# Attention two items at a time, with the softmax's reciprocals applied to its output

## The chip, the cores and the metric

The kernel runs on one core of a Trainium2 chip. The metric is the device time of one execution in microseconds. The profile is one execution taken by the hardware profiler; its engines are PE (matrix products), DVE (VectorE), ACT (ScalarE), POOL (GpSimd) and SP, which issues the transfers. PE has a second row in the profile, PEld, for its weight loads.

## The reference

Attention over 4 batches of 8 heads, 576 positions of 64 numbers, with rotary embedding of queries and keys; its output, as 2304 tokens of 512 numbers, goes through two dense blocks of 512 to 2048 to 512.

```python
q_rot, k_rot = rotate(q), rotate(k)
scores = q_rot @ k_rot.T / sqrt(64)
scores = scores - max(scores)                # per row
attn = exp(scores)
attn = attn / (sum(attn) + 1e-9)
x = (attn @ v) as (2304, 512)
h = x @ w1_in;  g = h if h > 0 else exp(h) - 1;  x = g @ w1_out
h = x @ w2_in;  g = h - tanh(h);                 out = g @ w2_out
```

All is float32.

## The kernel before, in words

**Attention** works on 16 pairs of heads. A pair is cut into nine items: for each of four blocks of 128 query rows (u = 0 to 3) one item for the first head (h = 0) and one for the second (h = 1), and a ninth item (h = None) that holds the last 64 rows of both heads. An item is 128 rows of 576 scores.

The loop (lines 377 to 409) takes one item a turn. In turn i it emits, in this order: loads that are due, the row maximum of item i on DVE (`emit_max`, line 216), copies out of PSUM that earlier transposes left (`flush`, lines 256 to 275, two of five on DVE, three on ACT), the scores of item i + 1 on PE (`emit_s`, line 207), the exponential of item i on ACT with the row sums as a by-product (`emit_exp`, line 230), the normalization of item i - 1 (`emit_norm`: an add of 1e-9 and a reciprocal on DVE, lines 242 and 243, and for each head a multiplication of 128 x 576 on POOL, line 246), preparation of the next pairs, the transposes of item i - 4 on PE (`emit_t`, line 293; a remainder of 64 columns of both heads together, line 307, or line 300 for the ninth item), and matmuls with v into the output (`emit_pv`, line 325). Outputs are made for row blocks 0 and 1, 2 and 3, and the ninth item, 256, 256 and 64 columns wide, in five chunks each. Every engine executes its own instructions in the order of emission.

**PSUM** has eight banks: two score tiles of two banks (`ps_s`), two tiles for transposes (`ps_t`), two for outputs (`ps_v`).

**Preparation** (`prep`, lines 132 to 163) turns the loaded q (x = 0) or k (x = 1) of a pair into a rotated copy, in five steps: two products with the tables of cosines and sines (POOL, line 142, for most), their sum (DVE, line 144), a rounded high half (ACT, line 147), and the low half, what the rounding left (DVE, line 152). Then `place` (lines 174 and 177) copies both halves by transfers on SP's queue to the tiles that the scores read: k in four copies, two for each head. A table (`early`, and the offsets in the line that makes `when`) says in which turn each step is emitted. For k the sum, the high half and the low half are due in turns 2, 3 and 4 of the pair before, and the scores of the pair's first two items are emitted in that pair's turns 8 and 9.

**Weights** of the dense blocks arrive as pairs of words and are converted in five parts (`conv_w`), for the first eight tiles during attention.

**The dense blocks** (from line 415) take 192 steps: 12 matmuls of `emit_f1` (line 442) and 12 of `emit_f2` (lines 498, 500) each, with activations, and splits into high and low halves on ACT and POOL, between them. They read the layer's input as a high half `xh` and a low half `xl`. Attention fills these directly: ACT rounds the output in PSUM to `xh` (line 273) and DVE subtracts to `xl` (line 265). Sums over the groups of the hidden dimension go to `acc`.

Of the kernel before, what the change touches and what calls it, by code (L numbers as in the profile page):

```python
# [8 lines left out]
F32 = mybir.dt.float32  # L9
# [14 lines left out]
def attention_elu_tanhshrink(ctx: ExitStack, tc: tile.TileContext, qk, v, w1i, w1o, w2i, w2o, tab, out):  # L24
# [22 lines left out]
    xh = const.tile([128, KC, NTOK], F32R, name="xh")  # L47
    xl = const.tile([128, KC, NTOK], F32R, name="xl")
# [52 lines left out]
    with ExitStack() as actx:  # L101
# [10 lines left out]
        tabs = acst.tile([128, 2, S], F32, name="tabs")  # L112
        zero = acst.tile([128, 64], F32, name="zero")
# [5 lines left out]
        def load_qk(p, x):  # L119
            if p == 1 and x == 0:  # L120
                t = p3.tile([128, 2, S], F32, tag="a", name="t0")
            else:
                t = (p1, p2)[x].tile([128, 2, S], F32, tag=f"t{x}", name=f"t{x}")
            nc.sync.dma_start(out=t, in_=qk[p, :, 2 * x:2 * x + 2, :])
            t_t[p, x] = t
# [6 lines left out]
        def prep(p, x, i):  # L132
            t = t_t[p, x]
            mul = SCALE if p > 0 and x == 0 else 1.0
            if i < 2:
# [4 lines left out]
                else:  # L140
                    eng = nc.vector if p < 2 and i == 1 else nc.gpsimd
                    eng.tensor_tensor(out=t[:, i, :], in0=t[:, i, :], in1=tabs[:, i, :], op=ALU.mult)  # L142
            elif i == 2:
                nc.vector.tensor_tensor(out=t[:, 0, :], in0=t[:, 0, :], in1=t[:, 1, :], op=ALU.add)  # L144
            elif i == 3:
                hl_t[p, x] = p1.tile([128, 2, S], F32R, tag=f"hl{x}", name=f"hl{x}")
                nc.scalar.mul(hl_t[p, x][:, 0, :], t[:, 0, :], mul)
# [87 lines left out]
        def emit_norm(i):  # L235
# [15 lines left out]
        late, late_x, late_l = [], [], []  # L251
# [4 lines left out]
        def flush():  # L256
# [7 lines left out]
            for x0, hp, o, n in late_l:  # L264
                nc.vector.tensor_tensor(
                    out=xl[:, hp, x0:x0 + n], in0=o[:, 0:n], in1=xh[:, hp, x0:x0 + n].bitcast(F32),
                    op=ALU.subtract,
                )
            late_l.clear()
            for p, grp, o, n in late_x:  # L270
                b, hp = divmod(p, 4)
                x0 = b * S + 256 * grp
                nc.scalar.copy(out=xh[:, hp, x0:x0 + n], in_=o[:, 0:n])
                late_l.append((x0, hp, o, n))
            late_x.clear()

        def emit_t(i):
# [3 lines left out]
            if (u % 2 == 0) and h in (0, None):  # L281
                if grp < 2:
                    aT_t[p, grp] = (p2.tile([128, 2, 4, 256], F32, tag="aT", name="aT"),
                                    p2.tile([128, 256], F32, tag="aTr", name="aTr"))
                else:
                    aT_t[p, grp] = (p1.tile([128, 2, 4, 64], F32, tag="aT2", name="aT2"),
                                    p1.tile([128, 64], F32, tag="aTr2", name="aTr2"))
# [6 lines left out]
            if h is None:  # L294
                for hh in range(2):
                    evac(aT[:, hh, :, 0:64], pt[:, :, 64 * hh:64 * hh + 64])
                pr = ps_t.tile([128, 4, 128], F32, tag="pt", name="pr")
                for hh in range(2):
                    sl = slice(64 * hh, 64 * hh + 64)
                    nc.tensor.matmul(out=pr[sl, 0, 0:64], lhsT=a[sl, 0, 512:576], rhs=ident[sl, sl],  # L300
                                     start=True, stop=True)
                evac(aTr[:, 0:64], pr[:, 0, 0:64])
                return
            evac(aT[:, h, :, q0:q0 + 128], pt)
            if h == 1:
                pr = ps_t.tile([128, 4, 128], F32, tag="pt", name="pr")
# [3 lines left out]
        o_t = {}  # L310

        def emit_pv(p, grp, c):
# [3 lines left out]
            if c == 0:  # L316
                o_t[p, grp] = ps_v.tile([128, 256], F32, tag="o", name="o")
# [298 lines left out]
```

## Time and profile before

| what | value |
|---|---|
| time, median of 3 runs | 1138.52 us (1137.78 to 1139.23) |
| time of the profiled execution | 1137.68 us |
| its span, from the first to the last instruction | 1135.9 us |
| TensorE clock granted | 1.00 |
| PE busy | 1100.1 us (97%) |
| DVE busy | 769.7 us (68%) |
| ACT busy | 689.3 us (61%) |
| POOL busy | 647.6 us (57%) |

Busy time is the time covered by an engine's records. Matmuls are pipelined, so that the records of neighbours overlap, and a matmul's end is modelled: for PE, the distance from one start to the next tells more than the length of a record. The shares are averages over attention, which ends at about 324.6 us, and the dense blocks after it.

### The profile page before, as it was taken

The numbers are of one execution on the slowest core, as the hardware profiler recorded it, in microseconds if no ns is written. First come the engines' busy times: TensorE is split into PE (matmuls) and PEld (weight loads), VectorE is DVE, ScalarE is ACT, GpSimd is POOL, SyncE is SP. The second block draws the span as 40 slices with busy tenths as digits, with TensorE's granted clock in tenths as the row PEclk, the third lists the DMA queues.
The fourth block names the chain that finished last, engine by engine and source line by source line (L and its number), as shares of the span: only waits on it lengthen the run. The fifth ranks groups of instructions, "written<-read, shape, count | busy, mean of one in ns | idle before, by whom it ended". The sixth has DMA issues, their size and how long they took to land.

```text
span 1135.9 us, 18496 instructions
## 1 busy us (share of the span) xinstructions
PE 1100.1 (97%) x6656; PEld 983.9 (87%) x6656; DVE 769.7 (68%) x1383; ACT 689.3 (61%) x1479; POOL 647.6 (57%) x585
## 2 busy tenths in 40 slices
PE   2899999999999999999999999999999999999998
PEld 1677777777789999999999999999999999999997
DVE  5998889888743434455445466677768777877665
ACT  3677777777634343333333344688888788877774
POOL 2877888778423333333333366676666666666443
PEclk9999999999999999999999999999999999999999
DMA  7767676766211111111111111111111111110102
GB/s 231 197 193 192 191 182 189 200 195 187 72 38 38 38 38 40 54 38 38 57 38 38 38 50 44 38 38 38 56 38 38 38 55 39 38 38 1 57 34 79
DMA packets 29627, 91.96 MB, mean 81 GB/s; under 512 B 4192, under 2 KB 4192, under 8 KB 29536
## 3 DMA queue, kind: packets, MB, share of 16 engines
q1 hardware_dynamic: 29536, 90.78, 27.8%
q8 instruction: 53, 0.87, 0.3%
q14 instruction: 38, 0.31, 0.1%
HBM read 57.74 MB, written 4.72 MB: 55 GB/s over the span
## 4 chain that ended last, share of the span: by engine, by line
PE 86%; DVE 10%; DMA 2%; ACT 1%; issue 1%; SPq 1%; DVEq 0%; ACTq 0%
PE h L442 36%; PE y L498 18%; PE y L500 18%; PE o L325 6%; PE s L207 5%; PE pt L293 3%; DVE nm L216 3%; DVE aT L260 2%; DVE hl L152 1%; DMA k<-hl 1%; DVE den L242 1%; DVE t L144 1%; DVE f L79 1%; PE pr L307 1%; DMA tabs<-in_tab 0%
## 5 line engine op out<-in xcount | busy, mean ns | idle before, releaser
L442 PE MATMUL h<-xh,w 128*128 128x384 f32 x1536 | 423.3, 336 | 0.0
L483 POOL TENSOR_TENSOR g<-f,g 128x384 fp32r<-128x384 f32 x192 | 214.9, 1120 | 232.5 <-ACT g L482 229.2
L442 PEld LDWEIGHTS h<-xh,w 128*128 128x128 f32 x1536 | 281.6, 188 | 3.8
L442 PE MATMUL h<-xl,w 128*128 128x384 f32 x768 | 258.3, 336 | 0.0
L498 PE MATMUL y<-g,w 128*128 128x384 f32 x1152 | 219.0, 339 | 0.0
L500 PE MATMUL y<-w,g 128*128 128x512 f32 x864 | 216.5, 395 | 0.0
L498 PEld LDWEIGHTS y<-g,w 128*128 128x128 f32 x1152 | 204.0, 188 | 0.0
L500 PEld LDWEIGHTS y<-w,g 128*128 128x128 f32 x864 | 161.6, 188 | 31.4
L246 POOL TENSOR_SCALAR a<-a,r 128x576 f32<-128x576 f32 x144 | 132.4, 932 | 70.5 <-DVE r L243 50.4
L459 POOL TENSOR_TENSOR w<-w,u 128x384 f32<-128x384 f32 x96 | 105.9, 1103 | 100.1 <-ACT w L458 100.1
L482 ACT CAST g<-f 128x384 fp32r<-128x384 f32 x192 | 97.9, 510 | 99.4 <-PE y L498 97.7
L442 PEld LDWEIGHTS h<-xl,w 128*128 128x128 f32 x768 | 144.2, 188 | 3.8
L470 DVE TENSOR_SCALAR f<-f 128x384 f32<-128x384 f32 x96 | 38.4, 400 | 153.9 <-ACT f L451 153.9
L451 ACT ACTIVATE f<-h 128x384 f32<-128x384 f32 x96 | 47.2, 492 | 150.0 <-PE h L442 146.4
L230 ACT ACTIVATE a<-s,nm 128x576 f32<-128x576 f32 x144 | 107.6, 747 | 39.6 <-DVE nm L216 31.7
L216 DVE TENSOR_REDUCE nm<-s 128x1 f32<-128x576 f32 x144 | 108.1, 751 | 32.4 <-PE s L207 31.6
L96 POOL TENSOR_TENSOR w<-f,w 128x512 fp32r<-128x512 f32 x64 | 82.7, 1292 | 54.2 <-ACT w L95 54.1
L517 DVE TENSOR_TENSOR acc<-y,acc 128x384 f32<-128x384 f32 (+1 forms) x126 | 74.0, 612 | 47.2 <-PE y L498 42.0
L474 DVE TENSOR_TENSOR f<-h,f 128x384 f32<-128x384 f32 x96 | 53.2, 554 | 71.4 <-ACT f L460 70.9
L476 DVE COPY_PREDICATED f<-mask,w 128x384 f32<-128x384 uint32 x96 | 91.7, 956 | 10.3 <-ACT g L482 0.5
L142 POOL TENSOR_TENSOR t<-t,tabs 128x576 f32<-128x576 f32 x59 | 88.1, 1494 | 15.6 <-DMA t<-in_qk 15.6
L293 PE MATMUL pt<-ident,a 128*128 128x128 f32 x576 | 89.0, 277 | 4.0 <-ACT aT L262 2.7
(58 smaller groups left out, 1479.5 us busy)
## 6 DMA issues: line engine op xcount, KB each, us to landing
k<-hl SPq DMA_DIRECT2D x64, 288.0 KB, 4.6
t<-in_qk SPq DMA_DIRECT2D x30, 576.0 KB, 4.8
raw<-in_w1i SPq DMA_DIRECT2D x16, 512.0 KB, 3.7
raw<-in_w1o SPq DMA_DIRECT2D x16, 512.0 KB, 3.7
raw<-in_w2i SPq DMA_DIRECT2D x16, 512.0 KB, 3.6
raw<-in_w2o SPq DMA_DIRECT2D x16, 512.0 KB, 3.6
v<-in_v SPq DMA_DIRECT2D x16, 288.0 KB, 5.1
qa<-hl SPq DMA_DIRECT2D x32, 144.0 KB, 2.3
```

Source lines behind the costliest of these rows:

```text
L142: eng.tensor_tensor(out=t[:, i, :], in0=t[:, i, :], in1=tabs[:, i, :], op=ALU.mult)
L216: nc.vector.tensor_reduce(out=nm, in_=s_t[i][:, :, 0:288], axis=AX.XY, op=ALU.max, negate=True)
L230: nc.scalar.activation(out=a.rearrange("p (x c) -> p x c", x=2), in_=s[:, :, 0:288], func=AF.Exp, bias=nm_t.pop(i), scale=1.0, accum_out=den,)
L246: nc.gpsimd.tensor_scalar(out=a, in0=a, scalar1=r[:, x:x + 1], scalar2=1.0, op0=ALU.mult, op1=ALU.mult)
L293: nc.tensor.transpose(pt[:, c, :], a[:, h or 0, c0:c0 + 128], ident)
L442: nc.tensor.matmul(out=hp, lhsT=w[:, wp, ws], rhs=x[:, c, xs], start=(m == 0), stop=(m == 3 * KC - 1))
L459: nc.gpsimd.tensor_tensor(out=w, in0=w, in1=u, op=ALU.mult)
L476: nc.vector.copy_predicated(f, mask.bitcast(U32), w)
L482: nc.scalar.copy(out=g[:, 0, :], in_=f)
L483: nc.gpsimd.tensor_tensor(out=g[:, 1, :], in0=f, in1=g[:, 0, :].bitcast(F32), op=ALU.subtract)
L498: nc.tensor.matmul(out=y_t[e][:, 0:NB], lhsT=w[:, wp, es], rhs=gt[:, gp, :], start=st, stop=sp)
L500: nc.tensor.matmul(out=y_t[e], lhsT=gt[:, gp, es], rhs=w[:, wp, :], start=st, stop=sp)
```

## The change

Attention takes two items a turn. A turn emits: loads; for each of the two items the reciprocals of the item two before it and its own maximum; two exponentials; the scores of the next two items; the copies out of PSUM; the multiplications of finished outputs; preparation; the transposes of the items three before; output matmuls. PSUM's banks become four for scores, three for transposes and one for outputs. The exponentials stay unnormalized: the reciprocals are spread over 64 columns for each head by POOL, transposed with the remainder, and multiplied into the output, which goes unrounded to `xa`, by DVE. `xa` serves as `acc` later. The split of `xa` into halves is made by `split_x` on ACT and POOL, for the first 384 tokens in attention's last turns, for the others in the first 20 steps of the dense blocks. The scale of q moves into a second table; the low halves of pairs after the first go to POOL, without a scale; loads of q come two turns earlier, into two buffers.

```diff
-    xh = const.tile([128, KC, NTOK], F32R, name="xh")
-    xl = const.tile([128, KC, NTOK], F32R, name="xl")
+    xa = const.tile([128, KC * NTOK], F32, name="xa")
+    x_t = {0: const.tile([128, 2, KC, NB], F32R, name="x0")}
+
+    def split_x(t, c):
+        a = xa[:, NTOK * c + NB * t:NTOK * c + NB * t + NB]
+        x = x_t[t]
+        nc.scalar.copy(out=x[:, 0, c, :], in_=a)
+        nc.gpsimd.tensor_tensor(out=x[:, 1, c, :], in0=a, in1=x[:, 0, c, :].bitcast(F32), op=ALU.subtract)
...
-        ps_t = actx.enter_context(tc.tile_pool(name="ps_t", bufs=2, space=PSUM))
-        ps_v = actx.enter_context(tc.tile_pool(name="ps_v", bufs=2, space=PSUM))
+        ps_t = actx.enter_context(tc.tile_pool(name="ps_t", bufs=3, space=PSUM))
+        ps_v = actx.enter_context(tc.tile_pool(name="ps_v", bufs=1, space=PSUM))
...
-                nc.vector.scalar_tensor_tensor(
-                    out=hl[:, 1, :], in0=t[:, 0, :], scalar=mul, in1=hl[:, 0, :].bitcast(F32),
-                    op0=ALU.mult, op1=ALU.subtract,
+                eng = nc.vector if p == 0 else nc.gpsimd
+                eng.tensor_tensor(
+                    out=hl[:, 1, :], in0=t[:, 0, :], in1=hl[:, 0, :].bitcast(F32), op=ALU.subtract
                 )
...
-            nc.vector.tensor_scalar_add(den, den, 1e-9)
+            rs = r_t[p, u] = sm.tile([128, 128], F32, tag="rs", name="rs")
+            for x in range(nh):
+                nc.vector.tensor_scalar_add(den[:, x:x + 1], den[:, x:x + 1], 1e-9)
             nc.vector.reciprocal(out=r[:, 0:nh], in_=den)
-            for x in range(nh):
-                a = a_t[p, u][:, x, :]
-                nc.gpsimd.tensor_scalar(
-                    out=a, in0=a, scalar1=r[:, x:x + 1], scalar2=1.0, op0=ALU.mult, op1=ALU.mult
-                )
+            nc.gpsimd.tensor_copy(
+                rs.rearrange("p (h d) -> p h d", h=nh), r[:, 0:nh].unsqueeze(2).broadcast_to([128, nh, 128 // nh])
+            )
...
+        def flush_o():
+            for p, grp, o, aTr, n in late_o:
                 b, hp = divmod(p, 4)
-                x0 = b * S + 256 * grp
-                nc.scalar.copy(out=xh[:, hp, x0:x0 + n], in_=o[:, 0:n])
-                late_l.append((x0, hp, o, n))
-            late_x.clear()
+                x0 = NTOK * hp + b * S + 256 * grp
+                for sl, r in ((slice(0, 128), aTr[:, 1, :]),) if grp < 2 else (
+                        (slice(0, 64), aTr[0:64, 0, 64:128]), (slice(64, 128), aTr[64:128, 0, 128:192])):
+                    nc.vector.tensor_tensor(out=xa[sl, x0:x0 + n], in0=o[sl, 0:n], in1=r, op=ALU.mult)
+            late_o.clear()
...
-                nc.tensor.transpose(pr[:, 0, :], a.rearrange("p h s -> p (h s)")[:, 512:640], ident)
-                evac(aTr[:, q0:q0 + 128], pr[:, 0, :])
+                nc.tensor.transpose(pr[:, 0:128], a.rearrange("p h s -> p (h s)")[:, 512:640], ident)
+                nc.tensor.transpose(pr[:, 128:256], r_t.pop((p, u)), ident)
+                evac(aTr[:, :, q0:q0 + 128], pr[:, 0:256].rearrange("p (x c) -> p x c", x=2))
...
-                when = [i0 + o for o in ((-8, -6, -4, -3, -2, -1), (-7, -2, 0, 2, 3, 4))[x]]
+                when = [i0 + o for o in ((-10, -6, -4, -3, -2, -1), (-7, -2, 0, 2, 3, 4))[x]]
...
+            nc.gpsimd.tensor_scalar(out=tabq, in0=tabs, scalar1=SCALE, scalar2=1.0, op0=ALU.mult, op1=ALU.mult)
...
+            emit_s(1)
+            for i0 in range(0, n + D + 3, 2):
+                both = (i0, i0 + 1)
...
+                for i in both:
+                    if 0 <= i - 2 < n:
+                        emit_recip(i - 2)
+                    if i < n:
+                        emit_max(i)
+                for i in both:
+                    if i < n:
+                        emit_exp(i)
+                for i in both:
+                    if i + 2 < n:
+                        emit_s(i + 2)
                 flush()
+                flush_o()
...
+                    if 0 <= i - D < n:
+                        emit_t(i - D)
...
+            if i < NJ * (NT - 1):
+                split_x(i // NJ + 1, i % NJ)
```

Here D is 3; it was 4.

## Rows read from the trace of the kernel before

**Rows 1.** Busy time by stretch, all engines: stretch, length, busy us (instructions), clock, DMA.
```profile
core 0: us, PE busy (x) PEld busy (x) DVE busy (x) ACT busy (x) POOL busy (x), PEclk, DMA share, GB/s
0.00:34.20 34.20, 11.09 (x46) 8.54 (x46) 22.58 (x32) 11.50 (x26) 12.07 (x16) 1.00 0.81 231
34.20:311.60 277.40, 269.14 (x2191) 198.88 (x2191) 244.13 (x505) 198.21 (x493) 215.23 (x199) 1.00 0.66 179
...
324.60:1135.90 811.30, 807.53 (x4316) 768.17 (x4314) 498.00 (x835) 474.04 (x947) 418.07 (x368) 1.00 0.14 42
```
**Rows 2.** Timeline of PE: start us, length of the merged run, instruction, count.
```profile
151.28 0.60 PE L293 MATMUL pt<-ident,a 128*128 128x128 f32 x4
151.72 0.27 PE L307 MATMUL pr<-ident,a 128*128 128x128 f32 x1
151.75 0.53 PE L207 MATMUL s<-k,qa 128*128 128x288 f32 x2
```
**Rows 3.** Timeline of PE, one pair's last items and the next outputs.
```profile
156.76 0.33 PE L300 MATMUL pr<-ident,a 64*64 64x64 f32 x4
157.02 1.52 PE L325 MATMUL o<-aT,v 128*64 128x256 f32 x12
158.47 0.80 PE L207 MATMUL s<-k,qb 128*128 128x288 f32 x4
159.10 0.60 PE L293 MATMUL pt<-ident,a 128*128 128x128 f32 x4
159.46 0.77 PE L207 MATMUL s<-k,qa 128*128 128x288 f32 x4
160.07 0.60 PE L293 MATMUL pt<-ident,a 128*128 128x128 f32 x4
161.17 0.33 PE L307 MATMUL pr<-ident,a 128*128 128x128 f32 x1 [0.51 <-DVE aT L260]
161.43 0.65 PE L325 MATMUL o<-aT,v 128*64 128x256 f32 x4
162.01 0.65 PE L325 MATMUL o<-aTr,v 64*64 64x256 f32 x4
162.59 0.69 PE L325 MATMUL o<-aT,v 128*64 128x64 f32 x16
163.21 0.33 PE L325 MATMUL o<-aTr,v 64*64 64x64 f32 x4
...
164.59 0.80 PE L207 MATMUL s<-k,qa 128*128 128x288 f32 x4
...
165.85 0.66 PE L293 MATMUL pt<-ident,a 128*128 128x128 f32 x4
```
**Rows 4.** Groups by line and shape, 34.2 to 311.6 us: count, busy us, mean ns, idle before.
```profile
L246 POOL TENSOR_SCALAR a<-a,r 128x576 f32<-128x576 f32 x137 | 127.3, 942 | 54.3 <-DVE r L243 34.2 <-PE s L207 10.1 <-PE o L325 2.5
L216 DVE TENSOR_REDUCE nm<-s 128x1 f32<-128x576 f32 x136 | 102.1, 751 | 29.2 <-PE s L207 28.4
L230 ACT ACTIVATE a<-s,nm 128x576 f32<-128x576 f32 x135 | 100.9, 747 | 31.8 <-DVE nm L216 24.0 <-DVE den L242 7.8
...
L142 POOL TENSOR_TENSOR t<-t,tabs 128x576 f32<-128x576 f32 x54 | 80.0, 1481 | 8.3 <-DMA t<-in_qk 8.3
...
L242 DVE TENSOR_SCALAR den<-den 128x2 f32<-128x2 f32 x60 | 26.0, 433 | 0.0
...
L147 ACT ACTIVATE hl<-t 128x576 fp32r<-128x576 f32 x28 | 19.1, 681 | 0.0
...
L262 ACT COPY aT<-pt 128x256 f32<-128x256 f32 x15 | 5.6, 373 | 3.5 <-DVE aT L260 3.5
```
**Rows 5.** Timelines of DVE, SP and PE around one pair's keys; line 174's landing times.
```profile
159.09 0.76 DVE L152 SCALAR_TENSOR_TENSOR hl<-t,hl 128x576 fp32r<-128x576 f32 x1
...
159.88 3.45 SPq L174 DMA_DIRECT2D k<-hl  x4
...
169.28 0.80 PE L207 MATMUL s<-k,qb 128*128 128x288 f32 x4
...
DMA to landing us min/median/max: 3.0/4.6/6.8
```

More of the change, by code (lines that the diff above doesn't have):

```diff
@@ L133, in prep @@
             t = t_t[p, x]
-            mul = SCALE if p > 0 and x == 0 else 1.0
             if i < 2:
@@ L146, in prep @@
                 hl_t[p, x] = p1.tile([128, 2, S], F32R, tag=f"hl{x}", name=f"hl{x}")
-                nc.scalar.mul(hl_t[p, x][:, 0, :], t[:, 0, :], mul)
+                nc.scalar.copy(out=hl_t[p, x][:, 0, :], in_=t[:, 0, :])
             else:
@@ L328, in emit_pv @@
             aT_t.pop((p, grp))
-            o_t.pop((p, grp))
+            done = (p, grp, o, aTr, n)
+            if grp == 1:
+                second.append(done)
+                return
             if grp == 2:
                 v_t.pop(p)
-            late_x.append((p, grp, o, n))
-        D = 4
+                late_o.append(second.pop())
+            o_t.pop((p, min(grp, 1)))
+            late_o.append(done)
+        D = 3
         NDIRECT = 2
@@ new lines, in attention_elu_tanhshrink @@
+            emit_s(1)
+            for i0 in range(0, n + D + 3, 2):
+                both = (i0, i0 + 1)
+                for i in both:
+                    for f, *arg in sched.get(i, ()):
+                        if f is not prep:
+                            f(*arg)
+                    if i == 1 or i % (2 * NI) == 12:
+                        load_w(first_w[nw.pop()]) if nw else None
+                for i in both:
[6 more added lines that the diff above has]
+                        emit_exp(i)
+                for i in both:
+                    if i + 2 < n:
+                        emit_s(i + 2)
+                flush()
+                flush_o()
+                for i in both:
+                    p, r = divmod(i, NI)
+                    if p < NPAIR:
+                        for f, *arg in sched.get(i, ()):
+                            if f is prep:
+                                f(*arg)
+                        c = NI * (p % 2) + r - 3
+                        if c >= 0 and c % 2 == 0 and c // 2 < NCV and p // 2 < len(first_w):
+                            key = first_w[p // 2]
+                            conv_w(key, key[2], c // 2)
+                for i in both:
+                    if 0 <= i - D < n:
+                        emit_t(i - D)
+                        pp, uu, hh = items[i - D]
+                        if uu in (1, 3) and hh == 1 or uu == 4:
+                            if uu < 4:
+                                last = i0 + 4
+                            for c in range(5):
+                                at = max(last, i0 + 2) if uu == 4 else i0 + 2 if c < 3 else last
+                                pend.append((at, pp, uu // 2, c))
+                for x in [x for x in pend if x[0] <= i0 + 1]:
@@ L408, in attention_elu_tanhshrink @@
                     emit_pv(*x[1:])
                     pend.remove(x)
+                for i in both:
+                    if n - 8 <= i < n and (i - n) % 2 == 0:
+                        split_x(0, (i - n + 8) // 2)
             while pend:
@@ L424, in attention_elu_tanhshrink @@
     ps_y = ctx.enter_context(tc.tile_pool(name="ps_y", bufs=4, space=PSUM))
-    acc = fcst.tile([128, KC * NTOK], F32, name="acc")
+    for t in range(1, NT):
+        x_t[t] = fcst.tile([128, 2, KC, NB], F32R, name=f"x{t}")
+    acc = xa
     b1 = fcst.tile([128, 1], F32, name="b1")
@@ L439, in emit_f1 @@
             ws = slice(128 * c, 128 * c + 128)
-            xs = slice(NB * t, NB * t + NB)
-            for wp, x in ((0, xh), (0, xl), (1, xh)):
-                nc.tensor.matmul(out=hp, lhsT=w[:, wp, ws], rhs=x[:, c, xs], start=(m == 0), stop=(m == 3 * KC - 1))
+            for wp, xp in ((0, 0), (0, 1), (1, 0)):
+                nc.tensor.matmul(
+                    out=hp, lhsT=w[:, wp, ws], rhs=x_t[t][:, xp, c, :], start=(m == 0), stop=(m == 3 * KC - 1)
+                )
                 m += 1
@@ L520, in emit_acc @@
                 if l == 0:
-                    xs = slice(NB * t, NB * t + NB)
-                    nc.scalar.copy(out=xh[:, e, xs], in_=a)
-                    nc.gpsimd.tensor_tensor(
-                        out=xl[:, e, xs], in0=a, in1=xh[:, e, xs].bitcast(F32), op=ALU.subtract
-                    )
+                    split_x(t, e)
                 else:
```

82 lines of the change are left out of this document (23 added, 59 removed).

## The prediction

> **What bounds the kernel now.** I read the stretches first, because the change touches only attention and the hand-over to the dense blocks. From 324.6 us on PE is busy 807.5 of 811.3 us [rows 1]: a change that adds no matmul there cannot shorten it, and the diff adds none. The stretch from 34.2 to 311.6 us runs from the scores of one pair's ninth item to those of the last pair's, 15 pairs: 277.40 / 15 = 18.49 us a pair, 2.05 an item. There PE is busy 269.1 of 277.4 us, DVE 244.1, POOL 215.2 and ACT 198.2. PE is nearest to full, but records of matmuls overlap, so I checked it in the order of its instructions, from start to start [rows 2, 3].
>
> The reader should see there that runs have fixed lengths. Twelve output matmuls take 1.45 us (157.02 to 158.47), the next two fours 0.58 each, the sixteen short ones 0.62. Four score matmuls take 0.63 and 0.61, the ten of the ninth item 1.26. Four transposes take 0.36 before scores and 0.44 before the remainder, which takes 0.03 before scores and 0.26 before an output. One run is longer: from 160.07 the four take 1.10, and the row after them names DVE's copy out of PSUM. Adding up a pair at fixed lengths: outputs 2 x (1.45 + 0.58 + 0.58) + 0.62 + 0.26 = 6.10 (the last 0.26 as for the four small transposes at 156.76); scores 8 x 0.62 + 1.26 = 6.22; transposes 4 x 0.36 + 4 x (0.44 + 0.03), for the ninth item 0.44 + 0.26, and 4 x 0.23 for the runs that turn to an output: 4.94. The sum is 17.26. So of 18.49 us PE waits only 1.23, or 19.7 us in 16 pairs. **That is all that better overlap in attention can win.**
>
> **The change part by part.**
>
> *POOL's normalization goes.* 144 instructions at 0.94 us [rows 4]. It ends no wait of PE's in the fixed-length sum, and the transposes run four items behind, so its removal is worth nothing by itself. What it costs instead is on PE: the reciprocals, spread to 128 x 128 by POOL, are transposed, five a pair. A transpose is 0.44 / 4 = 0.11 us, so 0.55 a pair, on the bound engine. The spread copy on POOL is not in the trace; between 0.1 and 0.94 us (the normalization is the nearest row, and 4.5 times as wide) I take 0.3, covered by POOL's new free time.
>
> *Order on PE.* Two items now: two score runs, then eight transposes, remainder and reciprocals. Before: 0.62 + 0.44 + 0.03 + 0.62 + 0.36 = 2.07. After: eight score matmuls take between 1.01 (eight tenths of the ten in 1.26) and 1.24, I take 1.15, since the run of ten is nearest in kind; ten transposes at 0.11 less the short last step are 1.02. Together 2.17, or 0.10 more; four times a pair, and 0.11 for the ninth item: 0.5 a pair more. PE's floor becomes 17.26 + 0.5 = 17.8.
>
> *DVE.* The low halves of q and k (two for each pair after the first, 0.76 in the row at 159.09 [rows 5]) move to POOL, where two-input work of this size takes 1.48 (line 142): 1.5 us a pair less on DVE. The adds on the sums of two columns average 0.43; by single columns they become 128 x 1, whose price I bound by 0.1 below and 0.43 above, and take 0.15, nearer to the lower end since half the columns are left: 9 x 0.15 instead of 4 x 0.43 + 0.15, 0.5 less. The multiplication of outputs replaces the subtraction of low halves, one piece more, and a wider copy of the remainder a narrow one: some 0.5 more, as an estimate from copies of 0.37 at 256 columns (line 262). So 1.5 us a pair goes from 16.3 (244.1 / 15), to 14.8. DVE isn't the bound, so this buys only punctuality. ACT loses the rounding of outputs.
>
> *Waits that go.* Scores take 0.80 to their end, the maximum 0.75 and the exponential 0.75 [rows 3, 4], so the scores of the next item but one may start 2.3 us after these, and a turn is 17.8 x 2 / 9 = 3.96 long. There are 1.6 us for the hand-overs and for lateness, where before each item had its own turn of 2.05. A third bank for transposes takes away waits like the one at 160.07.
>
> *Waits that stay or come.* First, in every second pair the last two items need four PSUM tiles out of three in one turn: the fourth waits for a copy, issued after two maxima; between 0 and 1.1 us (the longest such wait in the rows), I take 0.5, or 0.25 a pair. Second, the keys, below: 0.2 a pair on average.
>
> *One output bank.* An output of the next group is begun in the same turn in which DVE multiplies the former. Ahead of that multiplication stand two maxima (1.5), reciprocals and one or two copies; PE stands behind 2.2 us of scores and transposes of that turn, having started DVE's turn one turn earlier. I take nothing; lower bound nothing (no gain, since this only adds a wait), upper bound in the rivals. Here the Trainium skill speaks against the change: Perfetto Trace Analysis, section Optimizing Tensor Performance, Matmuls, says that independent groups should rotate through different PSUM banks so that emptying one overlaps with the next. No run of outputs in rows 3, which have two banks, is lengthened by such a wait, and with one bank there is no row yet; by that rule the time would be the third rival's.
>
> *Start and end.* The scaled tables put one 128 x 1152 instruction ahead of POOL's first product: 2 x 0.94 us as an upper bound, nothing as the lower; I take 1.0 us, since the first scores wait for that product. The layer input's split adds one ACT copy and one POOL subtraction per step in the first 20 steps, under PE's 811.3 / 192 = 4.2 us a step (ACT is busy 474 and POOL 418 us of that stretch [rows 1]): nothing while they keep up; if not, at most those few steps' lengths. DMA loads start two items earlier and hide as before.
>
> **Sum.** 16 x (1.23 - 0.5 - 0.45) = 4.5 us won, 1.0 lost at the start: 3.5. From the profiled execution's 1137.68 us (span 1135.9 and 1.8 around it; 0.8 under the median of the three runs): **1134 us**. A measurement of this kernel can tell about 0.2%, or 2.3 us.
>
> **The rivals.**
>
> *Slower: the keys come late.* This is the one that worries me. A pair's low half of k was subtracted by DVE at 159.09, its four copies issued from 159.88 over 3.45 us, and the second head's scores, which need the last one, ran at 169.28, 10.2 us after the subtraction began [rows 5]. Landing takes 4.6 (up to 6.8) from issue, the last issue is some 2.1 after the first: the keys are there 6.7 to 8.9 after the first issue. Now scores are emitted one item earlier, and for even pairs rounding and subtraction fall into one turn: after this turn's scores start, maximum to 1.6, two exponentials to 3.1, up to three copies of 0.37 to 4.2, rounding 0.68 (line 147) to 4.9, POOL's subtraction 1.48 to 6.4; keys at 13.1 to 15.3. The scores are due three turns later, 3 x 3.96 + 0.6 = 12.5, or 13.6 where two of the turns hold the longer outputs. Late by nothing to 2.8 us; seven even pairs after the first. In the sum it stands at 0.4 a time. If 1.5 to 2.8 decide, PE idles 10 to 20 us, less 3 already counted: **1141 to 1151**, around 1146. For it: the row's own slack was small. Against: k of the first head is due later than it lands, and turns with outputs stretch. It decides once keys land more than 1 us after their turn.
>
> *No change.* The 0.73 a pair that the floor allows is eaten by 0.7 of remaining waits: within 2.3 us of 1137.7.
>
> *Slower: DVE late at one bank.* POOL now runs more long instructions whose start DVE doesn't set, and something already holds DVE up there (0.43 us for an add of 128 x 2). If that makes DVE late by 0.5 us at each of 31 output tiles, PE loses 15 us: **about 1150**. It needs DVE's turn over 3.96 - 0.4; 14.8 x 2 / 9 = 3.3 speaks against it. The page of the Trainium skill named above tells of this outcome.
>
> *Faster by more.* If starts also get better (PE is busy 11.1 of the first 34.2 us, in which eight items' scores are done, 16.4 us at 2.05 each), up to 3 us come from there, and with no waits left 16 x 0.73 = 11.7: **1123 to 1130**.
>
> **How the numbers follow.** Forecast 0.42 (its own range 1130 to 1136), more 0.12, no change 0.16, late keys 0.22, late DVE 0.08. Faster by over 0.2%: 0.36 of the forecast's and 0.12, together 0.48. Within: 0.06 and 0.16, 0.22. Slower: 0.30. The range of 8 in 10 reaches from 1119 (the best of the fourth, with some microseconds for the fixed lengths read from few rows) to 1150.
>
> **What would show it.** Right: a pair period near 18.2 us, PE busy over 97% there; score runs in eights without a break; the time from 324.6 on unchanged at 811. Wrong in the step of the keys: scores of an even pair's second head preceded by a PE gap ended by the DMA of k, every second pair. Wrong at the bank: PE waiting for the multiplication before the first output matmul. Wrong altogether: a pair period under 17.5, which would mean that the fixed lengths weren't fixed but waits, or that scores in eights run faster than in fours.

## The result, and the profile after

The changed kernel takes 1144.95 us (median of 4 runs, 1144.12 to 1145.94), the one before 1138.54 beside it: a ratio of 1.0057 [1.0039, 1.0074], slower by 6.4 us. The prediction said 1134 us; the time lies inside its range, on the other side of the old one.

Busy time by stretch, of the kernel after, from its first ninth-item scores to the last and to the end of attention (columns as in [rows 1]):

```profile
core 0: us, PE busy (x) PEld busy (x) DVE busy (x) ACT busy (x) POOL busy (x), PEclk, DMA share, GB/s
0.00:34.76 34.76, 10.84 (x47) 8.14 (x47) 21.02 (x33) 10.69 (x24) 14.23 (x17) 1.00 0.76 221
34.76:316.07 281.31, 268.39 (x2233) 207.31 (x2234) 221.63 (x550) 186.83 (x452) 150.07 (x167) 0.99 0.65 178
316.07:330.04 13.97, 13.97 (x139) 9.42 (x137) 5.54 (x15) 5.55 (x13) 2.56 (x5) 1.00 0.01 2
330.04:1142.30 812.26, 808.56 (x4324) 769.20 (x4320) 507.56 (x836) 482.48 (x966) 439.40 (x388) 1.00 0.13 42
```

The second line answers to the second of [rows 1]: the 15 pairs take 281.31 instead of 277.40 us, 18.75 a pair instead of 18.49. DVE fell to 221.63 / 15 = 14.8 a pair, POOL from 215.2 to 150.1, ACT from 198.2 to 186.8, and the stretch got longer. The clock of 0.99 in this line comes from one place near its start: 0.81 was granted from 34 to 38 us and 0.54 from 38 to 40, near the lower of the two levels (1.2 GHz), after PE had stood idle for 2.16 us ahead of the scores at 34.76. By the rows this took about 1.6 us (an estimate: four transposes from 36.74 took 0.85 instead of 0.44, four scores from 38.73 1.11 instead of 0.63, and so on); the period counted below begins behind it, at 56.37. The dense stretch is 1 us longer (812.26 against 811.30); before, six matmuls of the first dense block stood among attention's last transposes, after, none does. So 5.4 of the 6.4 us are attention's.

Groups by line and shape of the kernel after, 34.76 to 316.07 us (columns as in [rows 4]):

```profile
L221 DVE TENSOR_REDUCE nm<-s 128x1 f32<-128x576 f32 x134 | 98.3, 748 | 17.7 <-PE s L212 17.3
...
L158 POOL TENSOR_TENSOR hl<-t,hl 128x576 fp32r<-128x576 f32 x28 | 39.7, 1418 | 25.2 <-ACT hl L152 25.2
...
L251 POOL COPY rs<-r 128x128 f32<-128x128 f32 x74 | 21.5, 290 | 79.9 <-DVE r L250 59.3 <-PE pr L305 14.2 <-PE pr L312 6.4
...
L249 DVE TENSOR_SCALAR den<-den 128x1 f32<-128x1 f32 x135 | 14.5, 144 | 0.2
```

The sizes that the prediction set are there: spread copy 0.29 us (0.3 was taken), single-column adds 0.144 (0.15), low halves on POOL 1.42 (1.48), DVE 14.8 a pair (14.8). The adds came out by luck: they are cheaper for another reason than half the columns (last section).

Timeline of PE in the kernel after, from one ninth item on:

```profile
148.22 0.80 PE L212 MATMUL s<-k,qa 128*128 128x288 f32 x4
148.86 0.79 PE L212 MATMUL s<-k,qb 128*128 128x288 f32 x6
149.48 0.79 PE L212 MATMUL s<-k,qa 128*128 128x288 f32 x4
150.10 0.60 PE L296 MATMUL pt<-ident,a 128*128 128x128 f32 x4
...
150.65 0.27 PE L312 MATMUL pr<-ident,rs 128*128 128x128 f32 x1
150.76 0.60 PE L296 MATMUL pt<-ident,a 128*128 128x128 f32 x4
152.22 0.79 PE L212 MATMUL s<-k,qb 128*128 128x288 f32 x4 [0.86 <-ACT a L235]
153.26 0.80 PE L212 MATMUL s<-k,qa 128*128 128x288 f32 x4 [0.24 <-ACT a L235]
153.89 0.60 PE L296 MATMUL pt<-ident,a 128*128 128x128 f32 x4
...
158.35 0.60 PE L296 MATMUL pt<-ident,a 128*128 128x128 f32 x4
159.44 0.33 PE L303 MATMUL pr<-ident,a 64*64 64x64 f32 x4 [0.49 <-DVE aT L266]
```

Two things repeat every two pairs. The turn that begins at 148.22 has no output run: its last four transposes go over to the next scores in 1.46 us where 0.36 to 0.48 is their length, and these scores need 1.67 to their transposes instead of 1.16. And from 158.35 four transposes take 1.09 instead of 0.53: the fourth PSUM tile of one turn, which the prediction named. PE's waits in the kernel after, 40 to 300 us (us in total, times, longest):

```profile
PE s L212 <- ACT a L235: 5.8, 9, 1.3
PE pr L303 <- DVE aT L266: 4.2, 7, 1.2
PE s L212 <- DMA k<-hl: 1.5, 1, 1.5
```

Scores wait for exponentials, remainders for a copy, once for keys. No output run waits for the single output bank. (This view counts the gap after a run's modelled end; from start to start it is more, 1.1 and 0.56 in the rows above.)

**A count of both kernels.** Over 14 pairs, between the sixteen short output matmuls of the first and of the 15th pair, the period is 18.46 us before and 18.80 after. With every run of matmuls at its usual shortest length, start to start, before comes to 16.93 a pair and after to 17.6, so PE waits 1.53 before and 1.2 after.

### The profile page after: what moved, and what is told of

Read it like the earlier page. It is cut to its first block, busy times and chain, and to the rows that moved or that the text cites. A ratio compares the mean times of both kernels' runs of the same rounds, so it can differ in the third digit from the quotient of the medians.

```text
span 1142.3 us, 18540 instructions
## 1 busy us (share of the span) xinstructions
PE 1101.8 (96%) x6736; PEld 994.1 (87%) x6736; DVE 755.8 (66%) x1433; ACT 685.5 (60%) x1455; POOL 606.3 (53%) x576
## 4 chain that ended last, share of the span: by engine, by line
PE 90%; DVE 5%; DMA 1%; issue 1%; POOL 1%; ACT 1%; SPq 1%; ACTq 0%; POOLq 0%
PE h L470 35%; PE y L528 18%; PE y L530 18%; PE o L331 7%; PE s L212 6%; PE pt L296 4%; DVE nm L221 2%; DMA k<-hl 1%; DVE t L149 1%; DVE aT L266 1%; ACT a L235 1%; PE pr L312 0%; PE pr L311 0%; DVE f L86 0%; DMA tabs<-in_tab 0%
## 5 line engine op out<-in xcount | busy, mean ns | idle before, releaser
L470 PE MATMUL h<-x,w 128*128 128x384 f32 x2304 | 433.7, 336 | 0.0
L470 PEld LDWEIGHTS h<-x,w 128*128 128x128 f32 x2304 | 407.2, 188 | 7.6
L221 DVE TENSOR_REDUCE nm<-s 128x1 f32<-128x576 f32 x144 | 105.8, 749 | 25.4 <-PE s L212 25.0
L547 DVE TENSOR_TENSOR xa<-y,xa 128x384 f32<-128x384 f32 (+1 forms) x126 | 74.0, 612 | 47.0 <-PE y L528 41.7
L486 ACT ACTIVATE u<-h 128x384 f32<-128x384 f32 x96 | 47.4, 494 | 68.1 <-PE h L470 52.7
L296 PE MATMUL pt<-ident,a 128*128 128x128 f32 x576 | 83.1, 276 | 0.0
L331 PE MATMUL o<-aT,v 128*64 128x256 f32 (+1 forms) x768 | 80.1, 337 | 0.0
L55 POOL TENSOR_TENSOR x<-xa,x 128x384 fp32r<-128x384 f32 x48 | 52.7, 1114 | 40.8 <-ACT x L54 40.5
L212 PE MATMUL s<-k,qb 128*128 128x288 f32 (+2 forms) x348 | 61.6, 304 | 10.3 <-ACT a L235 5.5
```

The lines of the kernel that those rows point to most:

```text
L212: nc.tensor.matmul(out=s[:, half, o0:o0 + n], lhsT=w, rhs=k[:, part, c0:c0 + n], start=(m == 0 and part == 0), stop=(m == len(terms) - 1 a ...
L221: nc.vector.tensor_reduce(out=nm, in_=s_t[i][:, :, 0:288], axis=AX.XY, op=ALU.max, negate=True)
L296: nc.tensor.transpose(pt[:, c, :], a[:, h or 0, c0:c0 + 128], ident)
L331: nc.tensor.matmul(out=o[sl, 0:n], lhsT=w, rhs=m, start=(c == 0), stop=(c == 4))
L470: nc.tensor.matmul(out=hp, lhsT=w[:, wp, ws], rhs=x_t[t][:, xp, c, :], start=(m == 0), stop=(m == 3 * KC - 1))
```

## The experiments

All edits are to the kernel after unless it says otherwise, and times are to be read by the ratio to the kernel before on the same chip (the kernel after has 1.0057). The first theory was that DVE is late in its queue; the second, formed later, that the turns are uneven and that DVE is stretched (its instructions take longer) beside POOL.

**1. Multiplication of the outputs after the preparation.**

```diff
                 flush()
-                flush_o()
                 for i in both:
...
                             conv_w(key, key[2], c // 2)
+                flush_o()
```

> The changed kernel with one edit: in each turn the multiplications of finished outputs are emitted after the preparation (sum, weight conversion) and not before it. Theory A (DVE is late in one turn of two pairs, because it stands waiting for the last output matmuls with the preparation and the next maxima queued behind): the gap of 0.93 us and the one of 0.5 us ahead of the scores, once every two pairs, go, and the time falls by 7 to 11 us from 1145, to 1134 to 1138. Rival (the late exponential has another cause, such as the keys or POOL): within 2.3 us of 1145.

1143.95 us, 1.0048 [1.0036, 1.0060]: the rival's number. In the turn without outputs the maximum came 2.02 us after the turn's first scores instead of 2.33 and the next scores 3.70 instead of 4.00, so 0.3 earlier, one for one, but no more, since the sum that moved up was stretched. DVE and POOL, timeline of this run:

```profile
147.45 1.50 DVE L149 TENSOR_TENSOR t<-t 128x576 f32<-128x576 f32 x1
...
146.94 1.41 POOL L147 TENSOR_TENSOR t<-t,tabs 128x576 f32<-128x576 f32 x1
```

The sum took 1.50 us beside POOL's product; in the kernel after its mean is 0.757.

**2. No fourth PSUM tile.** The ninth item's remainder goes into the eighth's tile where both fall into one turn.

```diff
-                pr = ps_t.tile([128, 512], F32, tag="pt", name="pr")
+                pr, at = rem.pop(p)
+                c0 = 256
+                if at != turn[0]:
+                    pr, c0 = ps_t.tile([128, 512], F32, tag="pt", name="pr"), 0
...
```

> The changed kernel with one edit: where the transposes of a pair's eighth and ninth item fall into one turn, the ninth item's remainder goes into the free columns of the eighth's PSUM tile, so that the turn needs three tiles and not four. Theory (the fourth tile waits for a copy): the gap of 0.5 us before the ninth item's remainder, once every two pairs, goes: 8 x 0.5 = 4 us, to 1141. Rival (the gap only moves to the scores behind it, which wait for an exponential anyway): 1145.

1140.32 us, 1.0016 [1.0007, 1.0024]. The waits ahead of the small transposes are gone: 4.6 us, 0.29 a pair, where the prediction had 0.25.

**3. No transposes of the reciprocals.** This leaves out the division: the outputs are multiplied by ones.

```diff
...
-                nc.tensor.transpose(pr[:, 128:256], r_t.pop((p, u)), ident)
-                evac(aTr[:, :, q0:q0 + 128], pr[:, 0:256].rearrange("p (x c) -> p x c", x=2))
+                r_t.pop((p, u))
+                evac(aTr[:, 0, q0:q0 + 128], pr[:, 0:128])
```

> The changed kernel without the transposes of the reciprocals: outputs are multiplied by a tile of ones, so the softmax is left unnormalized; reciprocals and their spreading are still computed, and the copies of the remainder are narrower. Theory (PE is the bound, each transpose costs its 0.11 us): 80 x 0.11 = 8.8 us less, up to 2 more from narrower copies: 1134 to 1137. Rival (DVE's lateness sets the turn and the transposes fill gaps): 1143 to 1145.

1138.30 us, 0.9997 [0.9988, 1.0006]: 6.7 us for 80 transposes and the narrower copies. Two items at a time with no reciprocals on PE are no faster than one item at a time, so the transposes explain the loss in size, but not why nothing was won: the prediction's own terms make that kernel 1134 - 80 x 0.11 = 1125.

**4. PSUM banks four, two, two.**

```diff
-        ps_t = actx.enter_context(tc.tile_pool(name="ps_t", bufs=3, space=PSUM))
-        ps_v = actx.enter_context(tc.tile_pool(name="ps_v", bufs=1, space=PSUM))
+        ps_t = actx.enter_context(tc.tile_pool(name="ps_t", bufs=2, space=PSUM))
+        ps_v = actx.enter_context(tc.tile_pool(name="ps_v", bufs=2, space=PSUM))
```

> The changed kernel with PSUM banks four, two, two: two output tiles, two for transposes. Theory (the third bank for transposes is needed in every turn of two items, the second one for outputs isn't): the remainder waits for a copy in nearly every turn, at least 0.5 us in 72 turns: 1175 or more. Rival (the single output bank is what makes PE or DVE wait): faster than 1145.

1234.32 us, 1.0836 [1.0808, 1.0864]. PE's waits, 40 to 300 us:

```profile
PE pr L311 <- DVE aT L266: 16.9, 16, 1.5
PE pt L296 <- DVE aTr L266: 13.6, 11, 1.8
PE pt L296 <- DVE aT L266: 12.3, 12, 1.2
```

The third transpose bank is worth 89 us in this order, net of whatever the output bank given back for it brought, which no row shows. The Trainium skill (Perfetto Trace Analysis, section Optimizing Tensor Performance, Matmuls) wants independent groups rotated through banks, so that emptying one overlaps with the next; the trace agrees for the transposes, where three tiles of a turn are begun within 0.7 us (150.10 to 150.76 above), and not for the outputs, which are a turn apart.

**5. Low halves back on DVE** (line 157: `eng = nc.vector`).

> The changed kernel with one edit: the low halves of q and k are subtracted by DVE again. Theory A (DVE's turn is the tight place): DVE gets 1.5 us a pair more, and the time rises by 2 to 10 us, to 1147 to 1155. Rival (the keys' way is the tight place, as the prediction's slower case had it): the keys come earlier or the same, and the time falls or stays, 1138 to 1145.

1148.55 us, 1.0079 [1.0064, 1.0094]: 2.5 us slower than the kernel after by the ratios, whose intervals overlap. Moving them to POOL seems to help on balance, by little.

**6. POOL normalizes again**, in the two-item order (reciprocals and their transposes out, DVE copies the outputs).

```diff
...
+            for x in range(nh):
+                a = a_t[p, u][:, x, :]
+                nc.gpsimd.tensor_scalar(
+                    out=a, in0=a, scalar1=r[:, x:x + 1], scalar2=1.0, op0=ALU.mult, op1=ALU.mult
+                )
...
```

> The changed kernel with the reciprocals undone: POOL normalizes the exponentials as before, outputs are only copied, no reciprocals are transposed; two items a turn and the banks stay. Theory (PE is the bound and the transposes of the reciprocals cost it about what leaving them out gave, 6.7 us): 1138 to 1140 while POOL keeps up. Rival (POOL, which also has the low halves now, comes late with the second item's normalization, two turns being too short): slower than 1145, up to 1165.

1153.34 us, 1.0117 [1.0101, 1.0134]. PE's waits, 40 to 300 us:

```profile
PE s L212 <- DMA k<-hl: 10.7, 9, 2.1
PE pr L302 <- DVE aT L267: 9.9, 7, 2.2
```

Here the keys do come late, 9 times: POOL's low halves now queue with its normalization. So the reciprocals on PE pay for themselves in this order as long as POOL has the low halves; two items a turn with the normalization on POOL and the low halves on DVE was not run.

**7. Weight conversion eight items later**, by itself and with run 2's edit.

> The changed kernel with one edit: the five parts of a weight tile's conversion, and the load of the next tile, are due eight items later, so that no part falls on DVE into the turns in which it multiplies the outputs of a second and a third row group. Theory A (DVE's queue makes the maximum late in those turns; the conversion's 0.68 and 1.45 us are part of it): 0.7 to 1.4 us go, once in two pairs: 1134 to 1139 against 1145. Rival (the turn is late for the three multiplications and the rotation's sum alone, or DVE is made late elsewhere instead): 1143 to 1146.

1156.52 us, 1.0151 [1.0133, 1.0170], and with run 2's edit 1150.49, 1.0094 [1.0078, 1.0111]. Both are slower than either side expected (up to 1146, and up to 1139). The conversion met other turns and made those late: new waits between twelve output matmuls and scores, 8.1 us in 13 places. Its last instruction on DVE (line 94) now took 1.782 us on average (40 to 300 us), for example 1.88 from 216.77, where POOL had begun a low half at 216.68. A shift of DVE's work to turns chosen without looking at POOL cost some 10 us here.

**8. DVE's sum of every second pair on POOL** (with run 2's edit), and then also one DVE copy a pair on ACT.

```diff
-                nc.vector.tensor_tensor(out=t[:, 0, :], in0=t[:, 0, :], in1=t[:, 1, :], op=ALU.add)
+                eng = nc.gpsimd if x == 0 and p > 0 and p % 2 == 0 else nc.vector
+                eng.tensor_tensor(out=t[:, 0, :], in0=t[:, 0, :], in1=t[:, 1, :], op=ALU.add)
```

> The kernel with the shared remainder tile (1140.3), and the rotation's sum of the queries of even pairs on POOL, which idles 3.3 us there. This sum (0.76 us on DVE) stands between the three multiplications and the late maximum. Theory A (each microsecond taken out of DVE's queue in that turn comes off the scores' wait, until the wait of 0.95 + 0.5 is used up): 7 or 8 x 0.7 = 5 us less: 1135. Rival (the exponentials are late because of ACT or the keys): 1139 to 1142.

1139.49 us, 1.0013 [1.0005, 1.0022]: the same as run 2. DVE and POOL, timeline of this run:

```profile
147.47 1.14 DVE L90 SCALAR_TENSOR_TENSOR f<-raw,f 128x512 uint32<-128x512 uint32 x1
...
146.63 1.44 POOL L147 TENSOR_TENSOR t<-t,tabs 128x576 f32<-128x576 f32 x1
```

POOL's product now started later, 0.10 us after the turn's first scores and not 1.19 before them, and DVE's conversion beside it took 1.14 instead of 0.68 us. With the copy on ACT too, expected at 1132 to 1135, it was 1142.38, 1.0026 [1.0016, 1.0037], worse; what took it there was not followed.

**9. The kernel before, with one DVE copy a pair on ACT.** Of 15 copies out of PSUM DVE takes five instead of six, and one remainder less a pair (28 become 14 between 40 and 300 us).

```diff
-                if ev[0] % 5 in (1, 3):
+                if ev[0] % 15 in (3, 5, 8, 11, 13):
```

> The kernel before with one edit: the copy out of PSUM that follows a pair's first item goes to ACT, for which DVE takes the one of its fourth item. In the kernel before the remainder after the second item waits for this copy on DVE, 0.65 us in 7 of 14 pairs and less in others. Theory (what this kernel could win is a wait for a copy, not a new order): 3 to 6 us less, 1133 to 1136. Rival (another copy takes its place): 1138 to 1139.

1128.67 us, 0.9910 [0.9896, 0.9923]: faster than both kernels by 10 and 16 us, and by more than the 3 to 6 us that the theory had. PE's waits, 40 to 300 us, first of the kernel before, then with the edit:

```profile
PE pr L307 <- DVE aT L260: 4.5, 9, 0.7
PE pt L293 <- ACT aT L262: 2.1, 6, 0.4
```

```profile
PE pr L300 <- DVE aT L260: 0.8, 1, 0.8
PE s L207 <- DMA qa<-hl: 0.7, 2, 0.5
PE s L207 <- ACT a L230: 0.3, 1, 0.3
PE s L207 <- DMA k<-hl: 0.2, 1, 0.2
```

The stall of [rows 3] at 161.17 is gone. The period is 17.95 a pair: the one-item order has the shorter floor, 16.9, and its named wait went with a few copies out of DVE's way. Which of them did it, and where the gain beyond the theory's 3 to 6 us comes from, is not shown: three of a pair's 15 copies changed engine at once (two to ACT, one to DVE), and DVE's second clamp of the conversion (line 79) fell from a mean of 1.348 to 0.796 us with them (40 to 300 us). The banks of the kernel after (four, three, one) in the one-item order were not tried.

**10. No DVE conversion in attention** (with run 2's edit). The weights of the first eight tiles stay unconverted.

```diff
+        elif part in (1, 2) and short[0]:
+            pass
+        elif part == 3 and short[0]:
+            raw_t.pop(key)
...
```

> The kernel with the shared PSUM tile (e2), and DVE's part of the weight conversion left out during attention (two instructions of some 0.7 us at one step and one each at two others, for eight weight tiles; the weights of the first eight tiles stay unconverted, so the output is not the layer's). It takes work off DVE and puts it nowhere, so nothing can collide with it. Theory (the waits that stay in the two-item order are maxima and copies that come late on DVE once every two pairs): the 8.9 us of waits between 40 and 300 us that e2 still had, ahead of scores and ahead of transposes, mostly go, and the time is 1133 to 1136 us, 4 to 7 below e2's 1140.3. Rival (PE's own order of short runs sets the turn, and DVE's lateness is only beside it): within 1.5 us of 1140.3. In both cases PE's fixed lengths stay near 17.6 to 17.9 us a pair, so that it stays above the 1128.7 of the one-item kernel with its copy moved to ACT.

1137.49 us, 0.9987 [0.9978, 0.9996]: 2.8 to 3.3 us, between the two theories. With the conversion out most of the waits still stood: in the turn without outputs the four transposes still took 0.86 to 1.38 us in five of seven places and over 2.2 in two. In the first four of the five that is some 0.5 less than 1.46, near the 0.68 of the conversion that was left out, so DVE's queue is part of the chain; but about 0.5 stayed there, and 0.5 more behind the scores. So a late DVE alone was not it, and the first theory fell. What the places had in common was the turn. Another order on DVE, with the maxima ahead of the sum and the conversion in that turn, was not tried.

**11. Short outputs into the empty turn.** Lengths of turns of the kernel after, from scores to scores:

| Start | PE's runs in the turn | us |
|---|---|---|
| 139.73 | scores, transposes, twelve output matmuls | 4.09 |
| 143.82 | scores, transposes, four and four, short outputs | 4.40 |
| 148.22 | ten and four scores, transposes, **no outputs** | 4.00 |
| 152.22 | scores, transposes, twelve | 4.30 |

```diff
-                                at = max(last, i0 + 2) if uu == 4 else i0 + 2 if c < 3 else last
+                                at = max(last, i0 + 2 + 2 * (pp % 2)) if uu == 4 else i0 + 2 if c < 3 else last
```

> The changed kernel, with the sixteen short output matmuls and the four after them (0.62 and 0.26 us) of every second pair issued one turn later, in the one turn of two pairs that has no output run. Theory (in that turn PE has only 2.9 us of its own between two score runs, while scores, two maxima and two exponentials take longer, so PE waits there some 1.0 us ahead of the next scores and 0.5 ahead of their transposes): 0.9 to 1.4 us less in each of 7 or 8 places, 7 to 10 us, so 1135 to 1138. The row of four transposes that goes over to scores (1.46 and more, 6 times between 40 and 300 us) is gone. Rival (DVE's queue is late whatever the turn, as the run without its conversion, which left most of the waits standing, does not support): the wait moves to the turn that lost the short outputs, or to the output bank, and the time stays within 2 us of 1145.

1143.27 us, 1.0036 [1.0022, 1.0050]: within the rival's 2 us.

> The same edit on the kernel with the shared PSUM tile. Theory: 7 to 10 us below its 1140.3, so 1130 to 1133, and the edits add, since one takes away a wait ahead of transposes and the other one ahead of scores. Rival: within 2 us of 1140.3. In both cases above the 1128.7 of the one-item kernel with its copy moved.

1137.96 us, 0.9998 [0.9989, 1.0007]. The waits in the empty turn went: in the second run's first cycles this turn, now with short outputs, ends after 3.92 us, and the turn that gave them fell to 3.53. But only some 2 us of the expected 7 to 10 were kept. In four of seven places a wait came back two turns later; DVE, POOL and PE, timeline of the second run, first one cycle of two pairs earlier, where nothing waited, then where the wait came back:

```profile
149.71 0.69 DVE L94 SCALAR_TENSOR_TENSOR f<-raw,f 128x512 uint32<-128x512 uint32 x1
...
149.75 1.92 POOL L147 TENSOR_TENSOR t<-t,tabs 128x576 f32<-128x576 f32 x1
```

```profile
186.43 1.92 DVE L94 SCALAR_TENSOR_TENSOR f<-raw,f 128x512 uint32<-128x512 uint32 x1
...
188.64 1.42 DVE L221 TENSOR_REDUCE nm<-s 128x1 f32<-128x576 f32 x2
...
185.01 1.42 POOL L158 TENSOR_TENSOR hl<-t,hl 128x576 fp32r<-128x576 f32 x1
186.38 1.42 POOL L147 TENSOR_TENSOR t<-t,tabs 128x576 f32<-128x576 f32 x1
...
188.07 1.52 PE L336 MATMUL o<-aT,v 128*64 128x256 f32 x12
190.32 0.79 PE L212 MATMUL s<-k,qb 128*128 128x288 f32 x4 [0.73 <-ACT a L235]
```

Here DVE's last conversion took 1.92 us: it began 0.05 us after POOL's product and ended at 188.35, 0.55 after that product (187.80). The two maxima behind it were 1.2 late, and PE's twelve output matmuls took 2.25 to the next scores instead of 1.45. One cycle earlier DVE was first, by 0.04 us, and its instruction took 0.69, POOL's product 1.92.

**12. The last two parts of the conversion out of POOL's way**, one turn later (with the edits of runs 2 and 11), **and no DVE conversion at all** (the weights of the first eight tiles unconverted again).

```diff
                         c = NI * (p % 2) + r - 3
+                        c = -1 if c == 6 else c - 2 * (c > 6)
```

> The kernel with the shared PSUM tile and the later short outputs (e15), and the last two parts of the weight conversion one turn later: DVE's last one (128 x 512, two inputs) and the rounding with POOL's subtraction. In e15 this DVE instruction took 1.92 us instead of 0.69 where POOL had started a product of 1.42 just before it, and the two maxima behind it came 1.2 us late (PE waited 0.80 ahead of the next scores, in four of seven places). One turn later POOL stands idle behind its spread copy. Theory (DVE's two-input instructions stretched beside POOL's, of which the change has two more a pair, make the maxima late): the waits of 0.80 and 0.20 go, 3 to 5 us, so 1133 to 1135. Rival (DVE's order is late there anyway): within 1.5 us of 1138.

1133.79 us, 0.9958 [0.9944, 0.9972], as the theory had it.

> The same kernel (e15) with DVE's conversion left out during attention, as in the run without conversion before (the weights of the first eight tiles stay unconverted, so the output is not the layer's). Theory: with neither the turn without outputs nor a stretched conversion left, PE's waits between 40 and 300 us fall under 5 us, and the time is 1131 to 1134; the two edits, 2.3 and 2.8 us by themselves, give more together than their sum. Rival (the chain from scores over maxima and exponentials is too long for two-item turns in other turns too): 1134 to 1136, no more than the sum of the two.

1132.06 us, 0.9948 [0.9936, 0.9961], as the theory had it. Groups by line of DVE, 40 to 300 us, first of run 11's second kernel, then with the last two parts one turn later:

```profile
L94 DVE SCALAR_TENSOR_TENSOR f<-raw,f 128x512 uint32<-128x512 uint32 x7 | 9.6, 1367 | 0.2
```

```profile
L94 DVE SCALAR_TENSOR_TENSOR f<-raw,f 128x512 uint32<-128x512 uint32 x8 | 5.5, 683 | 0.0
```

The same instruction, with the same work, takes half as long one turn later, and the kernel 4.2 us less; taking the conversion away altogether gives 1.7 more at most (the two intervals overlap). PE's waits with the two parts one turn later, 40 to 300 us:

```profile
PE s L212 <- DMA k<-hl: 1.0, 1, 1.0
PE s L212 <- ACT hl L152: 0.7, 1, 0.7
PE s L212 <- ACT aT L268: 0.3, 1, 0.3
```

No wait of scores for an exponential is left. The period is 18.14 us a pair, 17.6 of it PE's own. So the second theory holds: two items at a time in this schedule loses to PE's fourth tile and to a turn without outputs, and once that turn is filled to DVE beside POOL. With all three mended (4.7, 2.0 and 4.6 us by the ratios) it is faster than the kernel before by 4.8 us.

## Why the prediction went wrong

**What PE has to do: right in kind, a little short.** The prediction put the floor at 17.26 a pair and at 17.8 with the change, 0.5 more. Measured it is 16.93 and 17.6, 0.67 more. Before's floor was read too high mostly because the ninth item's turn to an output was counted twice, in its 0.26 and again among the four times 0.23. The scores in eights did as said (1.16 for 1.15).

**Waits that go and stay: here it failed.** Its sum had 0.45 us a pair of waits left, of 1.23. There were 1.2 left, of 1.53. The waits it named were there: the fourth tile at 0.29 a pair (0.25 said), the keys once in 14 pairs at 1.5 us, 0.1 a pair (0.2 said). What it left out is the rest, some 0.8 a pair. From start to start 0.6 of it stands in one place, the turn without outputs (8.3 us over the 14 pairs, the place where the keys came last not counted). One step of the prediction missed this, a second one what came next:

- *The mean turn instead of the shortest.* This is the step that failed, under "Waits that go". It set the 2.3 us from scores to the exponential against a turn of 3.96. That is an average: the outputs are handed out over the turns, and once in two pairs a turn has none. From 148.22 PE has 1.88 + 0.44 + 0.22 + 0.44 = 2.98 us to do there, and the chain from scores over DVE's queue to the next scores takes 4.0. DVE, timeline of the kernel after in that turn:

```profile
148.34 0.79 DVE L277 TENSOR_TENSOR xa<-o,aTr 128x256 f32<-128x256 f32 x3 [0.70 <-PE o L331]
149.16 0.76 DVE L149 TENSOR_TENSOR t<-t 128x576 f32<-128x576 f32 x1
149.83 0.68 DVE L90 SCALAR_TENSOR_TENSOR f<-raw,f 128x512 uint32<-128x512 uint32 x1
150.55 0.76 DVE L221 TENSOR_REDUCE nm<-s 128x1 f32<-128x576 f32 x1
```

  The maximum of scores that began at 148.22 starts at 150.55, behind three other jobs, the first of which waits for the outputs of the turn before. In the kernel before, two turns without outputs follow each other at the same place (144.56 and 145.75, 1.19 and 1.79 us), and DVE's maxima start there at 144.03, 145.83 and 147.72, with three or four other jobs between them; the change puts the maxima of two items behind all the other jobs of the turn before.
- *POOL's new instructions at nothing.* The prediction moved 1.5 us of low halves a pair from DVE to POOL, and its sum did not ask which of DVE's instructions run beside them; only its rival of the late DVE did, with a chance of 0.08. DVE's last conversion had a mean of 0.984 us before (40 to 300 us) and has 1.442 after. In the kernel after this is not yet part of the loss: DVE's total is the 14.8 that was said, and the runs of PE behind that conversion keep their lengths (twelve output matmuls from 155.08 to 156.52, 1.44). It counts once the turn without outputs is filled (run 11), and run 12 prices its place at 4.2 us.

**The rivals.** The time lies among those of the late keys (1141 to 1151), but for another reason: one wait for keys of 1.5 us in the rows of PE's waits, not seven; the mechanism showed only in run 6. The single output bank held no one up; DVE was late, as the rival at that bank had it, but at the maxima. "No change" came nearest in kind: it set 0.7 a pair of remaining waits against 0.73 that the floor allowed, where the count has 1.2 against 0.86. The start cost 0.56 (34.76 against 34.20), not 1.0.

**The sum.** Per pair 0.67 more work, 0.3 less waiting: 0.35 longer, which is 4.9 of the 6.4 us over the 14 pairs counted; the rest of attention lost 0.6 net (the first pair's short outputs came 5.2 us later, start and low clock included; from the 15th pair's to the dense blocks it took 10.4 instead of 15.0), the dense blocks 1.0. With the waits the prediction had counted on (0.54 left in run 12) the kernel takes the 1134 us it forecast; those waits needed three further edits.

## What to carry to other kernels

Check a chain of hand-overs against the shortest turn in the rows, not against the mean one, and list for each turn what PE has of its own. When work is moved from DVE to POOL, look at which of DVE's instructions start just behind it: a conversion of 0.69 us that began 0.05 us after a product of POOL's took 1.92. And before a reordering that adds work to the bound engine, try the smallest move that takes the named wait away: here another split of the copies between DVE and ACT brought 10 us, the reordering at its best 5.

## What the runs showed of the hardware

A DVE instruction with two tensor inputs (128 x 512) takes 0.68 us alone and up to 1.92 where POOL has just begun a product; it then ended 0.54 and 0.55 us after that product (runs 8 and 11). Where DVE began 0.04 us before, POOL's product took 1.92 instead of 1.42. So the one that starts first holds the other back, almost to its own end. The Trainium skill (SBUF — State Buffer, section Who interferes with whom) says that a DVE instruction with two SBUF inputs contends with a GpSimd instruction that reads SBUF, and that issue order decides who waits; the trace agrees, with these numbers and with 0.757 against 1.50 for the 128 x 576 sum. Maxima, which read PSUM, took at most 0.76 us throughout.

Instructions with one tensor input were held up as well: in the kernel after, the clamp of 128 x 512 words (line 86) took 1.51 to 1.54 us in the seven places of attention where a product of POOL's was running, and 0.43 without one.

The mean of 0.433 us for an add on 128 x 2 [rows 4] is of this kind too and not its price. Adds of the kernel before, DVE and POOL:

```profile
144.89 0.15 DVE L242 TENSOR_SCALAR den<-den 128x2 f32<-128x2 f32 x1
157.59 1.26 DVE L242 TENSOR_SCALAR den<-den 128x2 f32<-128x2 f32 x1
...
157.42 1.41 POOL L142 TENSOR_TENSOR t<-t,tabs 128x576 f32<-128x576 f32 x1
```

Two thirds of the adds on 128 x 2 took 0.15 to 0.17 us; the long ones, 0.51 to 1.44, all ran beside a product of POOL's. The adds on 128 x 1 in the kernel after were never held up: 0.135 to 0.156 us in all 144, also beside POOL's low halves (two from 161.58, beside the one from 161.12 to 162.55). So, as these rows read, the single columns saved DVE's waiting for POOL and not the second column.
